# Keys' transposes moved to another PSUM ring, 34 copies moved from VectorE to ScalarE, and a new written-out order, in a one-core gated-recurrence and low-rank mixer kernel

## The chip, the cores and the metric

One core of one Trainium2 chip runs the whole program in one launch. The metric is the device time of an execution in microseconds (us). TensorE does the matrix products, VectorE (DVE in the profile), ScalarE (ACT) and GpSimd (POOL) do the elementwise work, and the queue of SyncE (SP) issues most of the transfers.

## The reference

The reference has two stages. The first is a recurrence with a complex gate over 768 tokens, for 4 batches x 8 heads with head size 48. The second mixes tokens with a rank-32 product and channels with a two-layer perceptron of width 1536.

```python
def _attn_ref(q, k, v, a_re, a_im):            # (4, 8, 768, 48) each
    mag = np.sqrt(a_re * a_re + a_im * a_im)
    scale = np.minimum(mag, 0.999) / (mag + 1e-06)
    a_re_n, a_im_n = (a_re * scale, a_im * scale)
    ...
    for t in range(S):
        ar, ai = (a_re_n[:, :, t, :, None], a_im_n[:, :, t, :, None])
        new_re = ar * S_re - ai * S_im
        new_im = ar * S_im + ai * S_re
        kv = np.einsum('bhd,bhe->bhde', k[:, :, t], v[:, :, t])
        S_re, S_im = (new_re + kv, new_im)
        y[:, :, t] = np.einsum('bhd,bhde->bhe', q[:, :, t], S_re)

def _moe_ref(x, U, V, w_ch1, w_ch2):           # x = y as (4, 768, 384)
    xt = x.transpose(0, 2, 1)
    h = xt @ U @ V
    u = x + h.transpose(0, 2, 1)
    ch = np.maximum(u @ w_ch1, 0.0) @ w_ch2
    return (u + ch).astype(np.float32)
```

## The kernel before, in words

The tokens are cut into 24 chunks of 128 (6 for each batch). Gates are worked out in 12 groups of two chunks, the mixer in 12 pieces of two chunks, numbered m = 0 to 11.

- `gates(g)` turns the gate of group g into logarithms of its size and into angles (ScalarE's tables, with VectorE between). From group 3 on (`SPLIT`) the logarithms and the angles are split into two parts for TensorE: one copy in the rounded type, in the tile `GS` (L658 for 768 columns, L772 for 384), and the remainder by a subtraction after it. Products with constant matrices (`es ps`, `ef ps`, `tot`, `ph`) then sum the parts along the tokens.
- `prep(i)` weighs the queries and keys of chunk i, then turns queries and keys in the procedure `turn` (L841): 16 small products each, from two halves of the array's rows into two PSUM tiles `tr`. ScalarE copies each of the two tiles out into `QK` (L852).
- `chain(i)` does the level products `inner` (L888, L891) and `corners` (L952), the state's update `dk` (L977), and the output products `y` (L1008, L1016). From group 5 on the `inner` products of two chunks are issued together.
- `mixer(m)` does the rank products (`rank`, `mixed`), transposes the mixed rows (`uTp`, L1088) and copies them into `uT` (chunk 0 of the piece by VectorE, L1094; chunk 1 by ScalarE, L1092), then multiplies with the weights: `up` (L1103) and `down` (L1336) for m up to 6, a form with fewer products, `few` (L1202), from m = 7 on.

PSUM has four rings of two buffers each. Their tags are `T` (gates' sums, all `tr` tiles, `rank`, `mixed`, `uTp`), `A` (`inner`, `corners`, some of `fix` and `few`), `Y` (`dk`, `y`) and `M` (`up`, `down`, `few`). A product that takes a buffer waits until the readers of the tile two takes earlier in its ring are done.

Nothing is reordered when the kernel runs. Every operation has a place in the table `ORDER`, written out by hand for each engine, kind and rank, and `Plan.order` sorts by place, so every engine has one fixed queue. TensorE's operations carry a number `way` for the layout in which the array is cut: 0 for the whole array, 1, 3, 5, 6 and 7 for layouts of smaller parts (`turn` and `mixed` have 5, `dk` and the first part of `y` 3, `inner`, `corners` and the second part of `y` 1, `up`, `down` and `few` 0).

`SPARE` names places ahead of which TensorE is given products of the identity that nothing reads (L1485, `up<-ident` and `down<-ident`); they write PSUM tiles of the ring `M` that are not in use yet. A unit is 128 columns, and up to four units make one product.

Of the kernel before, what the change touches and what calls it, by code (L numbers as in the profile page):

```python
# [19 lines left out]
HC = CH // 2  # L20
# [19 lines left out]
        ("POOL", "load"): {0: [21], 1: [43], 1.5: [38], 2: [22]},  # L40
        ("DVE", "load"): {1: [68]},
# [6 lines left out]
        ("ACT", "gates"): {0: [1, 4, 2, 6, 7, 11, 12, 13, 14, 42, 35, 49, 57, 60], 1: [25, 27, 37, 39, 40, 41, 48, 50, 53, 52, 56, 59], 2: [122, 101,  # L48
# [10 lines left out]
        ("DVE", "gates"): {0: [5, 8, 9, 15, 17, 66, 16], 1: [29, 44, 45, 46, 47, 67, 63], 2: [110, 140, 146, 179, 142], 4: [276, 311, 326, 359, 338],  # L59
# [10 lines left out]
        ("ACT", "angles"): {0: [75, 84, 89, 92, 95], 1: [77, 99, 108, 113, 114], 2: [210, 228, 250, 242, 245, 246, 267, 272, 275], 4: [378, 398, 416,  # L70
# [5 lines left out]
        ("DVE", "angles"): {0: [76, 88], 1: [82, 105], 2: [215, 236, 251], 4: [383, 399, 417], 6: [589, 598, 599, 609, 624, 625, 642], 8: [695, 714,  # L76
# [5 lines left out]
        ("DVE", "prep"): {0: [87, 96, 106], 1: [109, 119, 135], 2: [232, 249, 254], 3: [264, 278, 308], 4: [358, 415, 419], 5: [401, 454, 472], 6:  # L82
# [160 lines left out]
def kernel(  # L243
# [24 lines left out]
    nc = tc.nc  # L268
# [36 lines left out]
    BITS = range(SPLIT[0])  # L305
    PUT = (0, 2), (4, 6), (8, 10)

    AT_ONCE = (0, 1, 2)
    WP = 768

    def pool(name, bufs=1, **kw):
# [1240 lines left out]
```

## Time and profile before

| | us |
|---|---|
| median of 3 runs (lowest, highest) | 637.16 (634.21, 637.46) |
| the profiled execution, its own time | 638.28 |
| its span, first to last instruction | 636.5 |
| busy: TensorE products (PE) | 621.5 (98%) |
| busy: VectorE (DVE) | 513.8 (81%) |
| busy: ScalarE (ACT) | 401.2 (63%) |
| granted TensorE clock, mean | 0.994 |

PE is the row of products, PEld that of the weight loads, which overlap them. The busy time of PE is modelled, and a product that follows another of the same form starts long before the one ahead of it has ended, so a busy PE can still hide short delays. A row of the timeline gives the start, the length from the first start to the last end, the engine, the line and the count; a row of the chain of waits gives the stretch by which this work moved the end of the chain on. A line L383, L386 or L380 is a helper's, and such rows are told apart by their tiles.

### The profile page before, as it was taken

The page shows a single profiled execution, that of the slowest core. Times are in us where ns is not written, and L with a number is a line of the kernel's source. Part 1 is how long each engine was busy: PE and PEld are TensorE (multiplying, and loading weights), DVE is VectorE, ACT ScalarE, POOL GpSimd, SP SyncE. Part 2 cuts the span into 40 slices and gives each one's busy share as a digit, 9 for nine tenths or more (in the row PEclk, how much of TensorE's full clock was granted, in tenths as well). Part 3 has the DMA queues.
Part 4 walks back from the last instruction along what each step waited for, and adds up shares of the span by engine and source line. Part 5 has one row for each costly group of instructions (what it writes and reads, how often), then busy time and mean ns, then how long its engine had stood idle before and what let it go on. Part 6 is the DMA issues. An engine that isn't in the chain of part 4 may idle for free.

```text
span 636.5 us, 23451 instructions
## 1 busy us (share of the span) xinstructions
PE 621.5 (98%) x10376; PEld 527.6 (83%) x10376; DVE 513.8 (81%) x921; ACT 401.2 (63%) x773; POOL 39.7 (6%) x79
## 2 busy tenths in 40 slices
PE   7999998999999999999999999999999999999998
PEld 3567667755889989889889889788999998999997
DVE  7999997799999989758877977888998985464643
ACT  7999987898887787876776675768532431202010
POOL 5000000001001000010010100010000000000010
PEclk9999989999999999999999999999999999999999
DMA  8865544537232452522422422512122110000011
GB/s 201 182 159 136 123 111 113 129 101 162 44 72 52 80 103 46 98 59 45 85 57 47 91 45 42 113 44 37 34 61 34 25 35 2 1 1 13 1 38 50
DMA packets 173685, 45.74 MB, mean 72 GB/s; under 512 B 167632, under 2 KB 170384, under 8 KB 173584
## 3 DMA queue, kind: packets, MB, share of 16 engines
q1 hardware_dynamic: 171376, 39.90, 29.8%
q0 software_dynamic: 2208, 4.35, 2.0%
q8 instruction: 81, 1.33, 0.9%
q14 instruction: 20, 0.16, 0.1%
HBM read 33.59 MB, written 4.72 MB: 60 GB/s over the span
## 4 chain that ended last, share of the span: by engine, by line
PE 83%; issue 5%; DVE 4%; ACT 4%; DMA 2%; SPq 0%; POOL 0%; DVEq 0%; ACTq 0%; POOLq 0%
PE down L1336 24%; PE up L1103 17%; PE few L1202 11%; PE tr L841 4%; PE dk L977 4%; PE y L1016 4%; PE inner L891 3%; PE y L1008 2%; PE inner L888 2%; PE up L1485 2%; PE tot L726 2%; PE mixed L1070 1%; ACT gate L380 1%; PE uTp L1088 1%; PE es ps L678 1%
## 5 line engine op out<-in xcount | busy, mean ns | idle before, releaser
L1103 PE MATMUL up<-uT,w 128*128 128x256 f32 x504 | 119.1, 388 | 0.0
L383 DVE TENSOR_TENSOR QK<-QK,T 112x512 f32<-112x512 f32 (+2 forms) x144 | 103.0, 732 | 11.2 <-PE inner L888 4.3
L1103 PEld LDWEIGHTS up<-uT,w 128*128 128x128 f32 x504 | 94.5, 192 | 13.1
L1336 PE MATMUL down<-w,h 128*128 128x192 f32 x396 | 74.3, 332 | 0.0
L380 ACT ACTIVATE gate<-gate 128x768 f32<-128x768 f32 (+1 forms) x89 | 70.5, 798 | 4.6 <-DMA gate<-in_a_im_dram 1.8
L852 ACT COPY QK<-tr 112x512 f32<-112x512 f32 x96 | 53.2, 585 | 28.3 <-PE tr L841 27.6
L1336 PEld LDWEIGHTS down<-w,h 128*128 128x128 f32 x396 | 64.0, 190 | 2.7 <-issue 1.7
L383 DVE TENSOR_TENSOR QKC<-qk,cs 128x768 f32<-128x768 f32 x48 | 45.6, 955 | 10.6 <-PE dk L977 5.6
L1210 ACT COPY h<-few 128x512 f32<-128x512 f32 x30 | 17.3, 586 | 53.9 <-PE few L1202 53.9
L386 DVE TENSOR_TENSOR xo<-down,xo 128x192 f32<-128x192 f32 (+1 forms) x79 | 30.4, 387 | 21.1 <-PE down L1336 21.0
L1336 PE MATMUL down<-stage 128*128 128x192 f32 x198 | 37.6, 331 | 0.0
L841 PEld LDWEIGHTS tr<-ident,QKC 64*112 64x112 f32 x768 | 26.0, 130 | 12.7 <-issue 5.2
L1202 PE MATMUL few<-gate,w 128*128 128x128 f32 x280 | 36.3, 277 | 0.0
L841 PE MATMUL tr<-ident,QKC 64*112 64x64 f32 x768 | 33.1, 222 | 1.9 <-ACT QK L852 1.7
L1278 POOL DMA_DIRECT2D out_dram<-xo x32 | 18.8, 608 | 254.7 <-DVE xo L386 143.6
L1202 PEld LDWEIGHTS few<-gate,w 128*128 128x128 f32 x280 | 34.0, 192 | 0.2
L1485 PE MATMUL up<-ident 128*128 128x512 f32 (+3 forms) x82 | 31.0, 488 | 2.3 <-POOL ident masks.py:199 1.4
L764 POOL DMA_DIRECT2D gate<-F x15 | 12.4, 827 | 325.2 <-DVE F L789 203.5
L1336 PEld LDWEIGHTS down<-stage 128*128 128x128 f32 x198 | 32.0, 190 | 0.7 <-issue 0.2
L380 ACT ACTIVATE h<-up 128x512 f32<-128x512 f32 x42 | 24.8, 596 | 11.2 <-PE up L1103 10.9
L377 ACT ACT_TABLE_LOAD x24 | 30.8, 1283 | 1.1 <-PEq L1536 0.7
L957 ACT COPY AT<-corners 32x128 f32<-32x128 f32 x96 | 24.3, 255 | 10.6 <-PE corners L952 9.2
(168 smaller groups left out, 1255.7 us busy)
## 6 DMA issues: line engine op xcount, KB each, us to landing
stage<-in_moe_w_ch_dram SPq DMA_DIRECT2D x12, 768.0 KB, 4.9
gate<-in_a_im_dram SPq DMA_DIRECT2D x24, 192.0 KB, 3.7
gate<-in_a_re_dram SPq DMA_DIRECT2D x24, 192.0 KB, 3.5
qk<-in_q_dram SPq DMA_DIRECT2D x24, 192.0 KB, 3.2
qk<-in_k_dram SPq DMA_DIRECT2D x24, 192.0 KB, 3.3
VP<-in_v_dram SPq DMA_DIRECT2D x24, 192.0 KB, 3.3
AT<-DG SPq DMA_DIRECT2D x96, 32.0 KB, 2.3
T<-E SPq DMA_DIRECT2D x48, 48.0 KB, 2.9
```

The lines of the kernel that those rows point to most:

```text
L377: ACT(1.37, rank, lambda: nc.scalar.preload_act_table_set(name), writes=[TABLE])
L380: return nc.scalar.activation(out=o, in_=i, func=f, **kw)
L383: nc.vector.tensor_tensor(out=o, in0=a, in1=b, op=OP.mult)
L386: nc.vector.tensor_tensor(out=o, in0=a, in1=b, op=OP.add)
L841: nc.tensor.transpose(out=get(*ps[r])[0:DQ, h], in_=get(*qkc)[at, h].rearrange("p u d -> p (u d)")[:, 0:DQ], identity=ident[at, at], tile_ ...
L852: nc.scalar.copy(out=to, in_=a)
L977: nc.tensor.matmul(out=get(*dk[r])[x:end, h], lhsT=get(*ks)[at, h, x // DP, 0:end - x], rhs=get(*VPi)[at, h], start=True, stop=True, tile_ ...
L1016: nc.tensor.matmul(out=get(*y[u])[side(r, u), p], lhsT=k_of(h, r * HC, HC), rhs=get(*(mid_G if r else ("G", i - 1)))[:, h], start=False, s ...
L1103: nc.tensor.matmul(out=get(*ps)[:, e], lhsT=w1[:, f, (ff + e) * 128:(ff + e + 1) * 128], rhs=get(*uT)[:, f], start=(f == 0), stop=(f == KD ...
L1202: nc.tensor.matmul(out=get(*ps)[:, q], lhsT=w()[:, q * 128:(q + 1) * 128], rhs=v[0](), start=(n == 0 and q == 0), stop=True, skip_group_ch ...
L1336: nc.tensor.matmul(out=get(*to)[:, part], lhsT=x(j), rhs=y[:, j], start=(first and j == 0), stop=(j == KH - 1), skip_group_check=not first)
L1485: nc.tensor.matmul(out=to[:, 0:k * 128].rearrange("p (k m) -> p k m", k=k), lhsT=ident, rhs=ident.unsqueeze(1).to_broadcast([128, k, 128]) ...
```

## The change

Four things are changed.

1. In `prep`, the two PSUM tiles of the keys' transposes come from the ring `A`; the queries' stay in `T`.
2. In `gates` and `angles`, the rounded copies into `GS` are made by ScalarE for groups 4 to 11 (8 copies of 768 columns, 16 of 384).
3. In `turned`, chunk 0 of the pieces m = 2 to 11 is copied into `uT` by ScalarE too (10 copies).
4. `ORDER` and `SPARE` are new as a whole. The set of operations is the same, apart from the engine of the 34 copies. `SPARE` has 127 units at 47 places where it had 120 at 36.

The code, and of the tables the rows of the transposes and the spare products:

```diff
-        ("PE", "prep"): {0: [107, 115], 1: [129, 148], 2: [260, 266], 3: [294, 319], 4: [420, 435], 5: [458, 480], 6: [725, 703], 7: [749, 776], 8:
-        [876, 913], 9: [927, 969], 10: [1059, 1078], 11: [1118, 1132], 12: [1305, 1299], 13: [1318, 1332], 14: [1452, 1473], 15: [1510, 1521], 16:
-        [1706, 1691], 17: [1739, 1727], 18: [1881, 1856], 19: [1911, 1895], 20: [2083, 2066], 21: [2096, 2110], 22: [2277, 2266], 23: [2290, 2297]},
+        ("PE", "prep"): {0: [115, 117], 1: [131, 153], 2: [268, 274], 3: [311, 310], 4: [419, 424], 5: [475, 476], 6: [730, 714], 7: [767, 768], 8:
+        [882, 914], 9: [921, 983], 10: [1073, 1084], 11: [1124, 1123], 12: [1299, 1271], 13: [1310, 1311], 14: [1470, 1477], 15: [1510, 1517], 16:
+        [1668, 1709], 17: [1708, 1736], 18: [1874, 1868], 19: [1905, 1899], 20: [2078, 2076], 21: [2105, 2104], 22: [2273, 2272], 23: [2302, 2304]},
...
-SPARE = {34: 19, 36: 1, 51: 11, 55: 2, 79: 7, 97: 1, 107: 9, 115: 2, 117: 3, 129: 1, 148: 14, 151: 2, 154: 2, 169: 1, 183: 1, 201: 2, 212: 4, 260: 6,
...
+SPARE = {33: 13, 34: 8, 50: 8, 85: 7, 115: 11, 128: 2, 151: 8, 153: 4, 172: 1, 179: 5, 202: 4, 224: 1, 237: 1, 242: 1, 246: 1, 247: 1, 249: 1, 268: 2,
...
     AT_ONCE = (0, 1, 2)
+    MADE = range(4, NG)
     WP = 768
...
                 a, b = ("gs0", g), ("gs1", g)
-                DVE(c_one(W), R1, lambda: nc.vector.tensor_copy(out=get(*a), in_=t(l)), [L], [a])
+                if g in MADE:
+                    ACT(ca, R1, lambda: nc.scalar.copy(out=get(*a), in_=t(l)), [L], [a])
+                else:
+                    DVE(c_one(W), R1, lambda: nc.vector.tensor_copy(out=get(*a), in_=t(l)), [L], [a])
...
                 a, b = ("zs0", g), ("zs1", g)
-                DVE(c_one(DM), R2, lambda: nc.vector.tensor_copy(out=of(a, i), in_=of(z, i)), [zi], [a + (i,)])
+                if g in MADE:
+                    ACT(c_act(DM), R2, lambda: nc.scalar.copy(out=of(a, i), in_=of(z, i)), [zi], [a + (i,)])
+                else:
+                    DVE(c_one(DM), R2, lambda: nc.vector.tensor_copy(out=of(a, i), in_=of(z, i)), [zi], [a + (i,)])
...
             for r in range(2):
-                psum(ps[r], "T", [128, H, HC])
+                psum(ps[r], "A" if u else "T", [128, H, HC])
...
-            if cc:
+            if cc or m > 1:
                 ACT(c_act(DM) - 0.045, R0, lambda: nc.scalar.copy(out=to(), in_=get(*tr)), [tr], [uT + (cc,)])
             else:
                 DVE(c_dve(DM), R0, lambda: nc.vector.tensor_copy(out=to(), in_=get(*tr)), [tr], [uT + (cc,)])
```

More of the change, by code (lines that the diff above doesn't have):

```diff
@@ L30 @@
 ORDER = {
[9 rows of a table removed]
-        ("POOL", "load"): {0: [21], 1: [43], 1.5: [38], 2: [22]},
-        ("DVE", "load"): {1: [68]},
[6 rows of a table removed]
-        ("ACT", "gates"): {0: [1, 4, 2, 6, 7, 11, 12, 13, 14, 42, 35, 49, 57, 60], 1: [25, 27, 37, 39, 40, 41, 48, 50, 53, 52, 56, 59], 2: [122, 101,
[10 rows of a table removed]
-        ("DVE", "gates"): {0: [5, 8, 9, 15, 17, 66, 16], 1: [29, 44, 45, 46, 47, 67, 63], 2: [110, 140, 146, 179, 142], 4: [276, 311, 326, 359, 338],
[10 rows of a table removed]
-        ("ACT", "angles"): {0: [75, 84, 89, 92, 95], 1: [77, 99, 108, 113, 114], 2: [210, 228, 250, 242, 245, 246, 267, 272, 275], 4: [378, 398, 416,
[5 rows of a table removed]
@@ L76 @@
-        ("DVE", "angles"): {0: [76, 88], 1: [82, 105], 2: [215, 236, 251], 4: [383, 399, 417], 6: [589, 598, 599, 609, 624, 625, 642], 8: [695, 714,
[5 rows of a table removed]
-        ("DVE", "prep"): {0: [87, 96, 106], 1: [109, 119, 135], 2: [232, 249, 254], 3: [264, 278, 308], 4: [358, 415, 419], 5: [401, 454, 472], 6:
[6 rows of a table removed]
-        ("ACT", "prep"): {0: [111, 112, 121, 120], 1: [141, 131, 149, 150], 2: [265, 261, 269, 270], 3: [298, 309, 324, 322], 4: [431, 430, 437, 438],
[4 rows of a table removed]
-        ("DVE", "rest"): {0: [116, 166, 171, 192, 134, 159, 176], 1: [177, 231, 238, 262, 214, 237, 243, 263], 2: [271, 321, 328, 355, 282, 295, 312,
[8 rows of a table removed]
@@ L103 @@
-        ("DVE", "levels"): {0: [128, 136, 167, 137, 144, 168], 1: [172, 190, 200, 185, 191, 223], 2: [274, 293, 327, 292, 303, 342], 3: [343, 361,
[9 rows of a table removed]
-        ("ACT", "levels"): {0: [147], 1: [211], 2: [313], 3: [379], 4: [470], 5: [508], 6: [769], 7: [851], 8: [948], 9: [1008], 10: [1160], 11:
[14 rows of a table removed]
-        ("ACT", "rest"): {0: [187, 204, 195, 194, 216, 218, 221], 1: [257, 255, 259, 268, 283, 285, 286], 2: [341, 332, 368, 363, 395, 389, 394], 3:
[10 rows of a table removed]
-        ("ACT", "small"): {0: [594, 291, 418, 489, 340, 521, 590, 593, 622, 630], 1: [748, 822, 791, 799, 771, 856, 878], 2: [985, 1087, 1141, 1121,
[4 rows of a table removed]
@@ L144 @@
-        ("DVE", "small"): {0: [244, 596, 631, 638, 644, 684, 685, 686, 602, 604, 741, 733], 1: [694, 734, 693, 830, 823, 852, 880, 904, 905, 920, 935,
[26 rows of a table removed]
-        ("POOL", "small"): {0: [1036, 870], 1: [1115, 1046, 1047], 2: [1408, 1257, 1310], 3: [1516, 1525, 1526], 4: [1703, 1688, 1719], 5: [2001,
-        1888, 2009], 6: [2140, 2080, 2141], 7: [2340, 2327, 2328], 8: [2638, 2635, 2666], 9: [2627, 2629, 2636], 10: [2628, 2634, 2637]},
-        ("POOL", "angles"): {6: [618], 8: [712, 736], 10: [873, 921], 12: [1114], 14: [1260, 1297], 16: [1467, 1500], 18: [1687], 20: [1889, 1921],
@@ L174 @@
-        22: [2045, 2068]},
-        ("DVE", "mixing"): {7: [2021, 2029, 2027, 2030, 2107, 2022, 2028, 2088, 2097, 2113, 2132, 2133, 2059]},
-}
-SPARE = {34: 19, 36: 1, 51: 11, 55: 2, 79: 7, 97: 1, 107: 9, 115: 2, 117: 3, 129: 1, 148: 14, 151: 2, 154: 2, 169: 1, 183: 1, 201: 2, 212: 4, 260: 6,
-         266: 2, 284: 2, 288: 1, 310: 1, 354: 1, 371: 1, 376: 1, 397: 1, 400: 2, 420: 1, 458: 2, 466: 3, 471: 4, 497: 1, 524: 1, 595: 3, 603: 2, 623:
-         3}
[9 rows of a table added]
+        ("POOL", "load"): {0: [16], 1: [31], 1.5: [28], 2: [27]},
@@ new lines @@
+        ("DVE", "load"): {1: [69]},
[6 rows of a table added]
+        ("ACT", "gates"): {0: [1, 2, 4, 6, 7, 10, 11, 19, 49, 35, 46, 47, 66, 67], 1: [23, 25, 39, 40, 42, 43, 48, 55, 52, 53, 54, 64], 2: [135, 111,
[10 rows of a table added]
+        ("DVE", "gates"): {0: [5, 8, 9, 12, 14, 59, 13], 1: [26, 21, 41, 44, 45, 70, 61], 2: [124, 139, 156, 194, 149], 4: [267, 319, 326, 353, 325],
[10 rows of a table added]
+        ("ACT", "angles"): {0: [68, 87, 101, 104, 105], 1: [79, 107, 113, 114, 125], 2: [212, 232, 252, 240, 241, 245, 261, 262, 264], 4: [380, 398,
[5 rows of a table added]
+        ("DVE", "angles"): {0: [77, 94], 1: [81, 108], 2: [217, 234, 255], 4: [386, 400, 412], 6: [585, 600, 604, 617, 621, 624, 637], 8: [698, 721,
[4 rows of a table added]
@@ new lines @@
+        ("DVE", "prep"): {0: [74, 106, 109], 1: [112, 130, 150], 2: [221, 253, 266], 3: [199, 296, 306], 4: [355, 410, 413], 5: [434, 452, 471], 6:
[6 rows of a table added]
+        ("ACT", "prep"): {0: [116, 121, 123, 122], 1: [145, 148, 157, 155], 2: [271, 272, 279, 278], 3: [320, 316, 315, 317], 4: [437, 438, 439, 440],
[4 rows of a table added]
+        ("DVE", "rest"): {0: [118, 154, 158, 185, 129, 184, 190], 1: [165, 208, 235, 263, 220, 243, 250, 254], 2: [283, 318, 328, 358, 280, 323, 341,
[8 rows of a table added]
+        ("DVE", "levels"): {0: [127, 133, 146, 132, 134, 152], 1: [173, 187, 188, 186, 189, 210], 2: [284, 292, 304, 291, 293, 309], 3: [329, 345,
[9 rows of a table added]
@@ new lines @@
+        ("ACT", "levels"): {0: [140], 1: [195], 2: [303], 3: [349], 4: [465], 5: [510], 6: [762], 7: [829], 8: [954], 9: [1014], 10: [1158], 11:
[14 rows of a table added]
+        ("ACT", "rest"): {0: [193, 191, 204, 192, 216, 226, 215], 1: [256, 258, 259, 257, 277, 275, 276], 2: [367, 340, 365, 366, 390, 391, 392], 3:
[10 rows of a table added]
+        ("ACT", "small"): {0: [595, 282, 312, 488, 393, 508, 607, 614, 622, 628], 1: [741, 808, 775, 813, 784, 847, 857], 2: [993, 956, 1110, 1142,
[4 rows of a table added]
+        ("DVE", "small"): {0: [248, 601, 632, 634, 642, 636, 679, 672, 609, 612, 743, 753], 1: [695, 747, 691, 836, 830, 831, 861, 873, 899, 916, 933,
[25 rows of a table added]
@@ new lines @@
+        ("POOL", "small"): {0: [816, 925], 1: [1113, 1103, 1163], 2: [1305, 1358, 1359], 3: [1511, 1474, 1516], 4: [1694, 1690, 1783], 5: [1975, 1886,
+        1976], 6: [2137, 2134, 2135], 7: [2363, 2282, 2372], 8: [2586, 2585, 2587], 9: [2641, 2588, 2628], 10: [2639, 2646, 2647]},
+        ("POOL", "angles"): {6: [620], 8: [713, 739], 10: [878, 930], 12: [1104], 14: [1267, 1307], 16: [1462, 1512], 18: [1676], 20: [1855, 1910],
+        22: [2020, 2091]},
+        ("DVE", "mixing"): {7: [2015, 2018, 2048, 2049, 2057, 2024, 2029, 2113, 2114, 2115, 2112, 2126, 2051]},
+}
@@ L183 @@
+SPARE = {33: 13, 34: 8, 50: 8, 85: 7, 115: 11, 128: 2, 151: 8, 153: 4, 172: 1, 179: 5, 202: 4, 224: 1, 237: 1, 242: 1, 246: 1, 247: 1, 249: 1, 268: 2,
+         274: 1, 281: 1, 285: 2, 286: 1, 310: 1, 336: 2, 338: 1, 344: 5, 369: 1, 376: 1, 378: 1, 394: 1, 408: 1, 418: 1, 419: 5, 424: 1, 431: 1, 442:
+         2, 469: 2, 472: 1, 503: 1, 519: 1, 596: 2, 602: 1, 610: 3, 619: 1, 623: 3, 627: 1, 640: 3}
 class Plan:
```

244 rows, old and new, of the table ORDER are left out of this document.

## The prediction

> **What bounds the kernel now.** I read first the busy time by stretches. Its columns are the stretch, its length, then busy us (and instructions) of PE, PEld, DVE, ACT and POOL, the granted clock, the DMA share and GB/s.
>
> ```profile
> 0.00:160.00 160.00, 148.90 (x2426) 98.67 (x2426) 142.15 (x234) 141.44 (x260) 12.39 (x35) 0.98 0.60 141
> 160.00:260.00 100.00, 99.69 (x2153) 88.83 (x2152) 94.33 (x162) 81.50 (x159) 5.79 (x9) 1.00 0.36 71
> 260.00:460.00 200.00, 199.39 (x3513) 174.22 (x3512) 159.60 (x280) 140.45 (x271) 13.97 (x21) 1.00 0.30 60
> 460.00:540.00 80.00, 80.00 (x1597) 73.67 (x1596) 66.43 (x132) 26.14 (x63) 2.72 (x5) 1.00 0.15 32
> 540.00:636.50 96.50, 93.48 (x697) 92.26 (x695) 51.25 (x116) 11.68 (x21) 4.80 (x9) 1.00 0.05 17
> ```
>
> There are two stages. Up to 160 us VectorE and ScalarE are each busy 88 to 89%, and TensorE idles 11.1 us although identity products fill another 31.0 us of it (L1485 among the costliest groups): here the elementwise work sets the pace. From 160 us to the last product TensorE idles about 1 us. The waits of PE from 160 to 633 us agree, they are three in all:
>
> ```profile
> PE inner L891 <- issue: 0.3, 1, 0.3
> PE y L1008 <- ACT gate L380: 0.3, 1, 0.3
> PE tr L841 <- ACT QK L852: 0.2, 1, 0.2
> ```
>
> So after 160 us only what shortens TensorE's own queue shortens the run. What its queue loses is not in idle time but in the products themselves. I read it in the chain of waits, in order of time (start, us, what):
>
> ```profile
> 160.92 1.07 PE dk L977 x57
> 161.99 0.59 PE tr L841 x16
> 162.58 2.79 PE up L1103 x12
> 165.37 0.35 PE ph L778 x2
> 165.72 2.59 PE up L1103 x12
> 168.31 0.59 PE tr L841 x16
> 168.90 0.62 PE inner L888 x51
> 169.52 2.79 PE up L1103 x12
> ```
>
> The same twelve products of `up` move the chain by 2.59 us behind whole-array work (`ph`) and by 2.79 us behind work in small parts (`tr`, `inner`). Coming back to the whole array therefore costs 0.20 us. Sixteen `tr` products take 0.59 us whether they follow `dk` or `up`.
>
> **Part 1, the order and the ring A.** I read TensorE's queue off both tables, operation by operation, with each one's `way`. The whole queue changes layout 282 times before and 264 times after. Up to the first `inner` of chunk 6 (160 us) both have 77 changes; from there on 205 become 187: into small parts from the whole array 77 to 74, back to the whole array 78 to 75, from one small layout to another 50 to 38. The reason is the ring: the keys' `turn` no longer needs the two T buffers that the queries' `turn` has just filled, and among the 34 `turn`s of the later stage there are now 13 places where two stand side by side, where there was none.
>
> Price of a change: back to the whole array 0.20 us (2.79 - 2.59). Into small parts: in the timeline the row of 16 `tr` products is 0.66 us long, its last product 0.22 us (the group's mean is 222 ns), so the 16 starts spread over 0.44 us, 0.03 us a step. A run behind its own kind would move the chain by 16 x 0.03 = 0.47 us, not 0.59: a change costs 0.12 us. Sum: 3 x 0.20 + (3 + 12) x 0.12 = 0.60 + 1.80 = **-2.4 us**, all of it on the path, since nothing else is awaited there. Bounds: if a second `turn` streams no faster than a first, the 12 changes between small layouts give nothing and -1.0 is left; if every change cost 0.20, -3.6. I take -2.4, the rows being of these very operations.
>
> Does the new ring add waits? `A` now carries 34 more tiles of the late stage. Their readers are two ScalarE copies of 585 ns (`QK`), `copy_predicated` of 294 and 443 ns, and four ScalarE copies of 255 ns (`AT`, 1.02 us together). Summing the rows of the TensorE work that stands between a tile's last product and the next take of its buffer, less its readers' rows, one take in `A` keeps 0.3 us to spare and all others over 1.2 us. In `T` the takes with under 1 us to spare fall from 44 to 24. So I put this at 0; if the cover went, a chunk would lose what its readers are late (the second rival).
>
> **Part 2, the start.** All `turn`s there and the spare products are re-placed. What the ring can save is seen in the waits of `tr`:
>
> ```profile
> PEld tr L841 <- ACT QK L852: 4.1, 9, 0.8
> ```
>
> Of the 4.1 us, 0.6 lie after 160 us, so 3.5 us at most in the start, behind ScalarE's copies of the queries. One of them has a sequel:
>
> ```profile
> 85.56 0.26 PE L841 MATMUL tr<-ident,QKC 64*112 64x64 f32 x1 [0.68 <-ACT QK L852]
> ...
> 86.64 4.54 PE L1103 MATMUL up<-uT,w 128*128 128x256 f32 x12
> ```
>
> That `up` is 1.7 us longer than the 2.86 us of the one at 162.51, in a stretch whose granted clock is 0.91. Bound of the gain: 3.5 + 1.7 = 5.2 us. But TensorE has slack here and VectorE and ScalarE do not, so a wait of TensorE that goes is mostly made up of waiting for them later. The three moved copies of group 4 fall in this stage: ScalarE gets 841 + 2 x 518 ns = 1.9 us, VectorE loses 558 + 2 x 355 ns = 1.3 us. From 120 to 160 us both are at 92% and more. The spare products grow by 7 units; 31.0 us for the bulk of 120 units is 0.26 us each, +1.8 us if they met no idle time, 0 if they do, as TensorE's 11.1 idle us let me expect. Bounds for the start: -5.2 to +3.7 us; I take 0, because elementwise work there changes by under 1%.
>
> **Part 3, copies after 160 us.** VectorE loses 7 x 558 + 14 x 355 + 10 x 552 ns = 14.4 us; ScalarE gains 7 x 841 + 14 x 518 + 10 x 478 ns = 17.9 us. The rows for VectorE, from the groups of instructions (busy us, mean ns of one, idle time before):
>
> ```profile
> L1094 DVE COPY uT<-uTp 128x384 f32<-128x384 f32 x12 | 6.6, 552 | 3.1 <-PE uTp L1088 3.1
> ...
> L772 DVE CAST GS<-gate 128x384 fp32r<-128x384 f32 x18 | 6.4, 355 | 2.9 <-DMA gate<-F 2.9
> ...
> L658 DVE CAST GS<-GL 128x768 fp32r<-128x768 f32 x9 | 5.0, 558 | 0.6 <-PE ph L778 0.3
> ```
>
> ScalarE's prices are from ACT rows of the same size (`gate` 768 columns 841, `cs` 384 columns 518, `uT` from PSUM 478). ScalarE is 70 to 82% busy from 160 to 460 us and can take this; VectorE's relief is worth nothing while TensorE does not wait for it. On the path is only `uT`: both halves now come one after the other, 2 x 478 = 0.96 us and not 0.55 side by side, so `up` or `few` gets its input 0.4 us later. Behind these copies on ScalarE stand the copies of `QK` and `h`; they wait with them if `uTp` is late. In the new order the TensorE work between the last `uTp` and the first product of `uT` is 0.9 to 1.0 us for m = 4 and 6 and 1.95 us (with VectorE's sums between) for m = 9 and 11; elsewhere it is 1.4 us and more. Four times up to 0.4 us: 0 to +1.6, I take +0.4.
>
> The Trainium skill speaks against this part: TensorEngine Tiling (Array Packing), section PSUM Bottleneck, asks for both ScalarE and VectorE to empty PSUM. By that rule all ten pieces would lose; the trace shows no product waiting for either copy (no waiter under L1092 or L1094), and which of the two holds here decides the third rival.
>
> **The sum.** -2.4 + 0 + 0.4 = -2.0 us. On the profiled execution, 638.28 us (span 636.5 and 1.8 around it), that is 636.3. The profile lies 1.1 us above the median, so the median goes from 637.16 to **635.1**; 0.5% is 3.2 us, about what a measurement of this kernel can tell from no change, so 634.0 and 640.3 are the bounds of "same".
>
> **The rivals.** *The start gets shorter too* (0.24). The waits behind `QK` and the half-speed stretch after them go, and VectorE and ScalarE follow: 4 of the 5.2 us, 631. For it: these waits are what the ring removes. Against: both engines are over 88% busy there.
>
> *The ring A holds TensorE up* (0.09, slower). Every chunk's keys wait in `A` for the readers of `corners` or `inner` on VectorE, 94% busy from 160 to 260 us. It decides from 5.2 us (2.0 + 3.2), 0.31 us for each of 17 chunks; at 0.5 us each it costs 8.5, giving 644. Against: the cover of 1.2 us and more.
>
> *The serial copies and ScalarE's load eat the gain* (0.16). Ten pieces at 0.4 us are +4.1 in place of +0.4, or the start pays ScalarE's 1.9 and part of the spare units: 637 to 639, no change.
>
> *Transposes side by side slow the clock* (0.03, slower). Thirteen pairs, each followed by a half-speed `up` at +1.7 us, 22 us, 657. The Trainium skill, TensorE: Matmul & The Clock Gate, Part 4, says that transposes do not count as busy for the gate. Against: a pair lasts 1.1 us, and the clock is 1.00 from 160 to 540 us with all its `tr`.
>
> **How the numbers follow.** The forecast itself has 0.48, its own range 633 to 637.5; about 0.14 of it lies under 634.0. Faster: 0.14 + 0.24 = 0.38. Slower: 0.09 + 0.03 = 0.12. Same: 0.34 + 0.16 = 0.50. The range that leaves out the slower cases and the lowest of the first rival is 630.5 to 640.0.
>
> **What would show it.** Right: from 160 us to the last product PE busy as before, 13 `tr` rows of x32 in the timeline, the stage about 2.4 us shorter, the start within 2 us of 160. Wrong: new waits of `tr` or `inner` on DVE or ACT rows after 160 us; `up` or `few` waiting for ACT `uT`; a `tr` x32 row longer than 1.2 us; a start that moved by more than 3 us, which would mean that I mis-sized the re-placed elementwise work.

## The result: 641.47 us, slower by 0.8%

After ran in 641.47 us (median of 10 runs, 638.82 to 642.85), before on the same chip in 637.29 us (10 runs). The ratio is 1.0078, 95% interval 1.0054 to 1.0101. The forecast was 635.1, its range 630.5 to 640.0. The profiled execution of after took 642.85 us, its span is 641.0.

First the same stretches as before, with two short ones of the start between them (stretch, length, busy us and instructions of PE, PEld, DVE, ACT and POOL, granted clock, DMA share, GB/s):

```profile
0.00:160.00 160.00, 144.19 (x2397) 99.00 (x2398) 135.46 (x225) 137.64 (x252) 12.15 (x34) 0.97 0.60 140
120.00:130.00 10.00, 7.33 (x102) 5.34 (x102) 5.71 (x10) 7.82 (x12) 0.00 (x0) 0.82 0.96 230
130.00:140.00 10.00, 8.81 (x54) 4.38 (x54) 4.55 (x9) 5.67 (x9) 0.96 (x1) 0.84 0.63 158
160.00:260.00 100.00, 98.64 (x2017) 85.80 (x2016) 88.81 (x148) 84.33 (x160) 6.03 (x9) 1.00 0.33 65
260.00:460.00 200.00, 199.99 (x3584) 176.14 (x3584) 155.17 (x266) 150.69 (x296) 13.46 (x21) 1.00 0.32 62
460.00:540.00 80.00, 80.00 (x1684) 75.20 (x1684) 68.08 (x136) 30.86 (x75) 3.84 (x7) 1.00 0.17 35
540.00:641.00 101.00, 97.97 (x738) 95.12 (x730) 51.61 (x117) 13.31 (x25) 4.83 (x9) 1.00 0.05 17
```

Up to 160 us VectorE has done 6.7 us less work and ScalarE 3.8 us less than in before (142.15 and 141.44). Most of the loss sits between 120 and 140 us: there VectorE is busy for 10.3 of 20 us, and TensorE's clock is 0.82 to 0.84. From 160 us on TensorE is as busy as before. Its waits from 160 us to the last product (one row, in place of three of 0.2 to 0.4 us):

```profile
PE ph L783 <- ACT QK L857: 1.4, 1, 1.4
```

To put a time on each stretch I gave every TensorE operation the time that it usually takes in before, and looked up when each profile has done the first so many us of that work. The table gives this as a difference from the profile of before (us; minus is earlier; 110 us of work are done at 164.5 us in before, 550 us at 616.3, and nothing changes after that). The rows below "after" are the experiments.

| work done | 50 | 70 | 90 | 110 | 230 | 410 | 550 |
|---|---|---|---|---|---|---|---|
| after | +3.1 | 0.0 | +6.1 | +8.4 | +7.3 | +4.5 | +4.5 |
| e1_late | -0.1 | -3.0 | -3.0 | +1.6 | -0.8 | -3.7 | -3.7 |
| e1_again | +0.2 | -2.8 | -2.8 | -0.6 | -2.8 | -5.7 | -5.7 |
| e2_start | +3.2 | +0.8 | +5.2 | +6.4 | +6.1 | +10.2 | +10.7 |
| e3_back | +3.1 | +0.5 | +6.1 | +9.1 | +8.4 | +16.6 | +16.9 |
| e4_r | +4.0 | +1.9 | +8.0 | +9.5 | +8.4 | +6.0 | +5.9 |
| e5_carry | +5.0 | +3.1 | +7.3 | +7.9 | +6.5 | +3.7 | +3.7 |
| e6_both | +3.1 | +1.3 | +3.3 | +5.4 | +4.5 | +1.7 | +1.6 |
| e7_split | 0.0 | -3.9 | -3.8 | -2.6 | +0.2 | +1.1 | +2.2 |
| e8_zs | -0.2 | -2.4 | -1.9 | -0.6 | -2.2 | -4.1 | -3.9 |
| e9_dve | -0.1 | -3.9 | -3.8 | -3.0 | -5.1 | +3.9 | +4.2 |
| e10_cover | 0.0 | -1.8 | -1.3 | +0.5 | -1.8 | -4.7 | -4.7 |
| e11_copies | -0.1 | -1.7 | -1.6 | +0.4 | +3.6 | +5.9 | +5.9 |
| f1_middle | +2.7 | +1.8 | +2.8 | +3.6 | +2.4 | -0.5 | -0.6 |
| f2_from585 | +0.6 | +3.0 | +8.3 | +9.7 | +7.4 | +4.5 | +4.4 |

So after loses 8.4 us in the start and gains 3.9 us between 110 and 410 us of work. The column at 110 depends on how the work is weighed: with the median step from one product's start to the next as its time, this column is 1.1 to 1.2 us lower for every kernel with after's late order (after +7.2, e1_late +0.4) and the same for e2_start and e11_copies, while the other columns agree within 0.5 us. By these weights the late gain of after is 2.7 us. (At 70 the kernels with before's start are 1.7 to 3.9 us ahead of before's own profile, which had a stretch at half clock at 111 us; differences of 2 us between single profiles mean little.)

A part is lost early. At 50 us of work (about 86 us in before) the seven kernels with after's first 584 places are 2.7 to 5.0 us behind, and all others within 0.6 us of before. In this stretch the new `SPARE` puts spare products ahead of products that are awaited (the same ten us of before and of after, then two rows of after's timeline):

```profile
70.00:80.00 10.00, 9.37 (x239) 6.23 (x238) 9.99 (x16) 9.50 (x22) 0.00 (x0) 1.00 0.60 125
70.00:80.00 10.00, 10.00 (x246) 6.95 (x245) 8.48 (x15) 8.04 (x18) 0.00 (x0) 1.00 0.54 122
73.94 1.24 PE L1490 MATMUL up<-ident 128*128 128x512 f32 x4
75.87 0.49 ACT L379 ACTIVATE gate<-ef ps 128x384 f32<-128x384 f32 x1 [0.85 <-PE ef ps L684]
```

After has 3.6 us of spare products here, before none. TensorE never idles, while VectorE and ScalarE do 1.5 us less each. The products `tot` of the third group start at 76.61 us in after and at 73.65 us in before. In the 5.3 us ahead of them stand four rows of spare products, which take 2.2 us of TensorE's queue. No run leaves these spare products out, so that they cost the 3 us is argued from rows and not shown.

The larger part is lost later, first on TensorE (timeline of after: start, us, engine, line, tiles, count, idle time ahead and its releaser):

```profile
121.75 2.14 PE L1056 MATMUL rank<-xo,UV 128*32 128x384 f32 x24
126.57 1.49 PE L1121 MATMUL rT<-fold,r 64*128 64x32 f32 x6 [2.67 <-ACT r L1062]
127.87 2.18 PE L1075 MATMUL mixed<-r,V 64*128 64x192 f32 x8
131.51 3.60 PE L1130 MATMUL rw ps<-w,rw 128*32 128x512 f32 x24
```

`rank` of piece 0 is done at 123.9 us, but its copy `r` stands in ScalarE's queue behind a weight conversion that waits for its load, so `rT` starts at 126.57 (before: 124.78). The two spare units placed ahead of `rT` are not issued, since the PSUM tiles that they would write are still to be read by copies of `h` that the new order has put later. Behind this idle stretch the clock is at half for 6.8 us (126.4 to 133.2 us in the trace's record of the clock): `rw ps` takes 3.60 us, in before 2.77.

Then the second wait (timeline of after, the rows around the carry row of chunk 6, which POOL's transfer adds to the first row of chunk 7's angles):

```profile
131.80 0.56 DVE L794 SCALAR_TENSOR_TENSOR F<-F,ph 128x384 f32<-128x384 f32 x1 [0.29 <-ACT F L379]
132.99 0.96 POOL L766 DMA_DIRECT2D gate<-F  x1 [120.69 <-DVE F L794]
133.29 0.37 SPq L550 DMA_DIRECT2D stage<-in_moe_w_ch_dram  x1
137.99 0.36 DVE L777 CAST GS<-gate 128x384 fp32r<-128x384 f32 x1 [4.76 <-DMA gate<-F]
```

The carry row is 1.5 KB. It is issued at 132.99, a weight load of 768 KB 0.30 us later, and `zs0` of chunk 7 can start 5.0 us after the issue; VectorE stands for 4.76 us with everything behind it. In before the weight load comes 1.29 us after the carry row (129.77 and 131.06), the row is there at 131.80 at the latest, and VectorE has `qk` of chunk 6 to do meanwhile. The trace's records of the DMA packets say where the time goes: the row's own packets begin 3.9 us after its issue in after, 1.5 us after it in before.

### The profile page after: what moved, and what is told of

Same layout as the page of the kernel before. It is cut to its first block, busy times and chain, and to the rows that moved or that the text cites. A ratio compares the mean times of both kernels' runs of the same rounds, so it can differ in the third digit from the quotient of the medians.

```text
span 641.0 us, 23499 instructions
## 1 busy us (share of the span) xinstructions
PE 620.8 (97%) x10400; PEld 531.3 (83%) x10400; DVE 499.1 (78%) x887; ACT 416.8 (65%) x807; POOL 40.3 (6%) x79
## 4 chain that ended last, share of the span: by engine, by line
PE 86%; ACT 4%; DVE 3%; DMA 3%; issue 2%; SPq 1%; ACTq 0%; DVEq 0%
PE down L1341 24%; PE up L1108 17%; PE few L1207 11%; PE dk L982 4%; PE tr L846 4%; PE y L1021 3%; PE inner L896 3%; PE up L1490 3%; PE y L1013 2%; PE inner L893 2%; PE down L1298 2%; PE tot L728 2%; ACT gate L379 2%; PE mixed L1075 1%; PE uTp L1093 1%
## 5 line engine op out<-in xcount | busy, mean ns | idle before, releaser
L1108 PE MATMUL up<-uT,w 128*128 128x256 f32 x504 | 116.2, 383 | 0.0
L857 ACT COPY QK<-tr 112x512 f32<-112x512 f32 x96 | 51.8, 592 | 16.8 <-PE tr L846 16.6
L1490 PE MATMUL up<-ident 128*128 128x128 f32 (+3 forms) x104 | 35.8, 448 | 1.4 <-POOL ident masks.py:199 1.4
L1097 ACT COPY uT<-uTp 128x384 f32<-128x384 f32 x22 | 10.1, 481 | 38.0 <-DVE more L1333 15.1
L908 DVE COPY_PREDICATED DG<-mask,inner 128x128 f32<-128x128 int32 (+1 forms) x72 | 23.8, 341 | 12.7 <-PE inner L896 6.2
L962 ACT COPY AT<-corners 32x128 f32<-32x128 f32 x96 | 24.3, 256 | 12.2 <-PE corners L957 10.7
```

Source lines behind the costliest of these rows:

```text
L857: nc.scalar.copy(out=to, in_=a)
L962: ACT(0.36, RR, lambda r=r, u=u: nc.scalar.copy(out=get(*ATi).rearrange("p (a u) t -> p a u t", u=2)[r:r + BLK, :, u, BLK:2 * BLK], in_=ge ...
L1108: nc.tensor.matmul(out=get(*ps)[:, e], lhsT=w1[:, f, (ff + e) * 128:(ff + e + 1) * 128], rhs=get(*uT)[:, f], start=(f == 0), stop=(f == KD ...
L1490: nc.tensor.matmul(out=to[:, 0:k * 128].rearrange("p (k m) -> p k m", k=k), lhsT=ident, rhs=ident.unsqueeze(1).to_broadcast([128, k, 128]) ...
```

## The experiments

The theory: the loss is the new order of the start, between 120 and 157 us, the gain of the late stage is real and comes from fewer changes of layout. Medians of runs on the same chip as before's; the ratios, with their 95% intervals, are to before, and are not exactly the quotients of the two medians.

**e1_late and e2_start: the halves.** e1_late has before's order up to place 740 and after's behind it; e2_start the opposite.

```diff
 e1_late, against after (and before's order up to place 740)
-    MADE = range(4, NG)
+    MADE = range(5, NG)
-                psum(ps[r], "A" if u else "T", [128, H, HC])
+                psum(ps[r], "A" if u and i >= 7 else "T", [128, H, HC])
 e2_start, against after (and before's order from place 740 on)
-    MADE = range(4, NG)
+    MADE = (4,)
-                psum(ps[r], "A" if u else "T", [128, H, HC])
+                psum(ps[r], "A" if u and i < 7 else "T", [128, H, HC])
-            if cc or m > 1:
+            if cc:
```

> The first 740 places in the order of before with its spare products, with all transposes of chunks 0 to 6 in ring T and group 4 copied by VectorE as before; everything after place 740 in the order of after, with the keys of chunks 7 to 23 in ring A and the copies of groups 5 to 11 and of uT for m = 2 to 11 on ScalarE. Theory (the loss lies in the new order of the start, between 120 and 157 us, and the late stage of after gains 3 to 4 us by fewer changes of layout): this kernel keeps the gain without the loss, 633.5, some 3.8 under before, range 632 to 635. Rival S (the late stage of after only makes up slack that its late start gave it): 637, as before. Rival R (ring A or the copies on ScalarE cost time late, and the start is a symptom): 640 to 641, as after.

> The complement: the first 740 places in the order of after with its spare products, keys of chunks 0 to 6 in ring A and group 4's copies on ScalarE; everything after that in the order of before, keys in T, copies on VectorE. Theory: the loss of the start (8.3 us at 157 us) without the gain of the late stage, 644 to 646. Rival S: the late stage makes up some 4 of the 8 us in either order, 641. Rival R: the late stage is as before, 637.

Measured: e1_late 633.99 us (before 637.94), ratio 0.992 (0.9893 to 0.9947); e2_start 646.38 us, ratio 1.0121 (1.0083 to 1.0158). Both as the theory had it (e2_start 0.4 us above its range): the halves go apart in opposite directions, -0.8% and +1.2%. Not all of e2_start's loss is the start. Its profile, of the slowest of its nine runs (649.07), is 6.4 us behind at 110 us of work and loses some 4 us more near 405 us, where TensorE waits 1.4 us for a placing transfer (`AT<-DG`) and the clock is then at half for 6.8 us. That the late stage only makes up slack (S) and that ring or copies cost time late (R) are both out.

**e3_back: all 34 copies back on VectorE, order and ring as in after.**

```diff
-    MADE = range(4, NG)
+    MADE = ()
-            if cc or m > 1:
+            if cc:
```

> The order, the spare products and the ring A of after, but all 34 copies back on VectorE at the same places in the order. Theory: the copies are off the path, 641 within 1.5 (group 4's copies stand after the place of the loss; the serial copies of uT cost at most 0.4 us each in four pieces, so at best 1.6 less). Rival R (ScalarE's extra load of 1.9 us in the start and 17.9 us late is what after pays): 637.

Measured: 652.62 us, ratio 1.022 (1.0184 to 1.0257), 1.4% over after. Neither theory had this: the copies are not indifferent, their move to ScalarE is needed by the new order. By the table 7 us of it are lost in one place, between 250 and 270 us of work, where `zs0` of chunk 16 waits in VectorE's queue for its carry row. e8_zs and e9_dve below take this up.

**e4_r, e5_carry, e6_both: the two waits repaired one by one.** Only the queues named change. In them `cx` and `w2` are conversions of weights, `h` is a copy out of `up`, `r` the copy out of `rank`, and `zs0` and `zs1` are the rounded copy and the remainder of a chunk's angles:

```diff
 e4_r, ScalarE's queue behind y of group 3
-  cx 9, r, n 8, w2 9, x 8, h(0,8), F 6, table, h(0,10), ...
+  h(0,8), h(0,10), r, cx 9, n 8, w2 9, x 8, F 6, table, ...
 e5_carry, VectorE's queue behind F 6
-  w2 9, zs0 7, zs1 7, h(0,0), ...
+  zs0 7, zs1 7, w2 9, h(0,0), ...
 e6_both: e4_r's queue, and VectorE's behind F 6
-  w2 9, zs0 7, zs1 7, ..., prep 6 qk
+  prep 6 qk, zs0 7, zs1 7, w2 9, ...
```

> After with one repair in ScalarE's queue: the copies h of piece 0 (rows 8 and 10) and then the copy r stand ahead of the weight conversion cx 9, which waits 1.3 us for its load, so r ends near 125.4 instead of 126.5 and the spare products ahead of rT find their PSUM tiles free. Theory: r 1.1 us earlier, no idle stretch of 3 us on TensorE and so no half-speed stretch of 6.8 us behind it (rT, mixed and rw ps cost 1.9 us more there): 2 to 3 us less at 132 us. If the carry row's transfer then no longer meets the weight load, up to 6 us less. 636 to 639 in the end. Rival C (the carry transfer that waits behind the weight load at 133 us sets everything, and what comes ahead of it has slack): 641.

> After with one operation moved in VectorE's queue: the weight conversion w2 that frees the stage buffer now stands behind the pair zs0, zs1 of chunk 7, which waits for the carry row (1.5 KB from POOL). The 768 KB weight load, which needs that buffer and was issued 0.3 us after the carry row's transfer, then comes 5 us later. Nothing else is moved, so VectorE still waits. Theory K (the carry row is slow because the weight load is in the DMA engines with it): from POOL's issue to zs0 about 2.5 us in place of 5.0, zs0 at 135.5 in place of 138.0, and 2 to 3 us less in the end: 638 to 640. Rival (the row takes 5 us by itself in this order, or the wait has slack behind it): 641 to 642.

> After with the moves of e4_r and e5_carry together, and the product of queries and keys with es (prep 6, 0.95 us) put ahead of zs0 of chunk 7 as cover on VectorE. Theory (two waits one behind the other: r behind the weight conversion, then the carry row behind the weight load): the first mixer's steps come 1.3 us earlier by the one and 2.5 us earlier by the other, and 0.9 us of VectorE's work fits into what is left: 4 to 5 us less than after, 636.5 to 638. Rival (each repair only uncovers the next wait, as e4_r did): 640 to 642.

e4_r: 642.30 us (before 637.94), ratio 1.0067 (1.0035 to 1.0098): nothing gained, rival C. Its timeline:

```profile
126.49 0.70 PE L1505 MATMUL down<-ident 128*128 128x256 f32 x2 [0.88 <-ACT h L394]
127.35 0.85 PE L1136 MATMUL rT<-fold,r 64*128 64x32 f32 x6 [0.16 <-ACT r L1077]
138.25 0.36 DVE L792 CAST GS<-gate 128x384 fp32r<-128x384 f32 x1 [4.84 <-DMA gate<-F]
```

The spare products are there again and `rT` runs at full speed, but `zs0` of chunk 7 starts at 138.25, as late as in after, 5.1 us behind its transfer's issue. The first wait had the second behind it.

e5_carry: 639.72 us (before 635.69), ratio 1.0063 (1.0036 to 1.009). Its timeline:

```profile
134.38 0.96 POOL L781 DMA_DIRECT2D gate<-F  x1 [122.88 <-DVE F L809]
136.38 0.36 DVE L792 CAST GS<-gate 128x384 fp32r<-128x384 f32 x1 [2.63 <-DMA gate<-F]
137.25 0.95 DVE L584 SCALAR_TENSOR_TENSOR w<-stage,w 128x768 uint32<-128x768 uint32 x1
138.26 0.37 SPq L565 DMA_DIRECT2D stage<-in_moe_w_ch_dram  x1
```

With the weight load 3.9 us behind it the carry row takes 2.0 us, not 5.0, and its packets begin 1.5 us after the issue, as in before. That settles the mechanism K, for the weight load together with the transfers behind it in SyncE's queue, which came later with it. What VectorE does meanwhile is not the cause: in before it works through the whole transfer, which is as short. The time follows in the profile alone (this execution came 1.9 us later to the place than after's, and left it 0.5 us earlier); the ratio can't be told from after's.

e6_both: 638.65 us (before 635.69), ratio 1.0045 (1.0018 to 1.0072). The carry row takes 2.0 us again (132.60 to 134.60), `zs0` starts 3.4 us earlier than in after, and the profile ends 2.9 us earlier. The forecast of 4 to 5 us was too much, and 5.4 of the 8.4 us at 110 us of work are still there. The interval of the ratio overlaps that of after (1.0054 to 1.0101), so the gain is read from the profile.

**f1_middle and f2_from585: where the rest is.**

```diff
 f1_middle
+  after's order to place 584, before's from there to its place 740, after's behind it
-    MADE = range(4, NG)
+    MADE = range(5, NG)
 f2_from585
+  before's order to place 585, after's behind it
-                psum(ps[r], "A" if u else "T", [128, H, HC])
+                psum(ps[r], "A" if u and i >= 5 else "T", [128, H, HC])
```

> After, with its order replaced only in the middle: places 0 to 584 as after (to 122 us, with SyncE's 14.2 us behind a placing transfer at 102 us), then what before has up to its place 740, then the order of after; group 4's copies on VectorE, all keys in ring A. Theory (the 8 us are lost in the order of places 585 to 740: the carry row behind the weight load, r behind the conversion, and what stands behind them): as e1_late, 0.992 to 0.997 of before, 632 to 635. Rival P (the loss is prepared before 122 us, by the weight loads that come 13 us late): 638 to 642.

> The complement: before's order up to place 585, after's from there on, copies on ScalarE from group 4 on, keys of chunks 5 to 23 in ring A. Theory: the loss is in it, 1.004 to 1.010 of before, 639 to 643. Rival P: 632 to 635.

f1_middle: 638.08 us (before 637.49), ratio 1.0009 (0.9991 to 1.0028). f2_from585: 640.98 us, ratio 1.0056 (1.0032 to 1.0079). f2 is as the theory had it: with before's first places, places 585 to 740 alone carry a loss. f1 missed the theory's range and lies at the lower end of P's: with before's middle after's first 122 us still cost 0.6 to 0.9% against e1 (0.992 and 0.995). Its interval lies under that of after, so the middle costs time too, and P holds in part. The parts don't add up: 0.006 to 0.009 for the early part alone, 0.011 to 0.014 for the middle alone, 0.013 to 0.016 for both. In f1's trace ScalarE still waits 1.4 us for a weight load at 132 us. Which operation before 122 us costs the time was not taken apart; it stays open. The table dates its loss: f1 is 2.7 us behind already at 50 us of work, where the rows above show the spare products. In the trace of after SyncE's queue stands, later than that, for 14.2 us behind a transfer that places level products (until 102 us, and the weight load behind it is issued at 107.2 where before issued it at 94.3).

**e7_split: 13 pairs of transposes separated again,** one of each pair moved past one or two neighbouring TensorE operations in e1_late.

```diff
 TensorE's queue, for instance chunk 7
-  tr(7,0), tr(7,1), up(1,0), ...
+  tr(7,0), up(1,0), tr(7,1), ...
```

> The kernel of e1_late with 13 pairs of transposes side by side separated again (chunks 7 to 23): one of each pair is moved past one or two neighbouring products of TensorE, nothing else. TensorE's queue changes layout 287 times in place of 264: 5 more into small parts from the whole array, 5 more back, 13 more between small layouts. Theory (the late gain of 4.2 us is TensorE's changes of layout): 5 x 0.20 + 18 x 0.12 = 3.2 us more than e1_late, 636.5 to 638. Rival (the late gain comes from the copies that left VectorE): within 1 us of e1_late, 633.5 to 635.

Measured: 645.07 us (before 635.69), ratio 1.0128 (1.0088 to 1.0169), 1.8 to 2.1% over e1_late, about four times the forecast. Its five runs fall into 640.4 (two) and 645.1 (three), and the profile is of one of the short ones (640.45). From 110 us of work to the end the profile loses 4.8 us where e1_late gains 5.3. Some 4.7 us of these 10.1 are idle time of TensorE (longest row below); it is the sum of 100, 100, 100 and 80 us less the busy time from 160 to 540 us, 4.74, against 0.06 in e1_late. The other 5.4 us, where 3.2 were forecast, lie in busy time and were not traced to rows. The moved transposes came too late for their readers:

```profile
PE inner L911 <- DVE QK L397: 2.5, 2, 1.6
```

So this run can't give the price of a change. The rows do: from the start of the last product ahead to the first behind it, a run of 16 `tr` between two `up` takes 0.90 us in before, a run of 32 takes 1.35 us in after, and an `up` follows another by 0.22 us (2.59 / 12). Two runs cost 2 x (0.90 - 0.22) = 1.37 us, one double run 1.13: a pair saves 0.24 us; 13 pairs would save 3.1 us, an estimate, since the other pairs stand between other products. The second 16 of a double run add 0.45 us (1.35 - 0.90).

**e8_zs and e9_dve: which copies the new order needs.** Both are e1_late with copies back on VectorE: all but `zs0` in e8_zs, `zs0` too in e9_dve.

```diff
 e8_zs
-                if g in MADE:
+                if 0:
                     ACT(ca, R1, lambda: nc.scalar.copy(out=get(*a), in_=t(l)), [L], [a])
-            if cc or m > 1:
+            if cc:
 e9_dve, on top of it
-    MADE = range(5, NG)
+    MADE = ()
```

> The kernel of e1_late with only the 14 copies zs0 of groups 5 to 11 still on ScalarE; the 7 copies of 768 columns (gs0) and the 10 of uT are back on VectorE at the same places. e3_back, with all 34 back, lost 11 us against after, 7 of them where zs0 of chunk 16 stood 3.3 us in VectorE's queue for its carry row, ahead of the state's update. Theory Z (it is the wait for the carry row that must not stand in VectorE's queue; gs0 and uT are of no account): 634 to 635.5. Rival (VectorE's load as such, or uT side by side, decides): 639 to 645.

> The kernel of e8_zs with its last 14 moved copies, zs0 of groups 5 to 11, back on VectorE too, so that only the order and the ring A are left of the late stage's change. Theory Z (with zs0 on VectorE the wait for the carry row stands ahead of the state's update in VectorE's queue and TensorE waits for that, then runs at half clock): 5 to 11 us more than e8_zs, 639 to 645, the loss at chunk 16 as in e3_back. Rival (e3_back lost by gs0 and uT, or by the start): within 1.5 us of e8_zs, 633 to 636.

e8_zs: 634.47 us (before 635.69), ratio 0.9981 (0.9946 to 1.0015); its profile gains what e1_late's does, but the ratio is not clear of 1. e9_dve: 643.87 us (before 636.96), ratio 1.0129 (1.0078 to 1.018), 1.5% over e8_zs. The loss is where theory Z put it. Timeline of e9_dve, then its stretch from 310 us:

```profile
309.55 0.36 DVE L791 CAST GS<-gate 128x384 fp32r<-128x384 f32 x1 [3.43 <-DMA gate<-F]
309.82 0.55 DVE L399 TENSOR_TENSOR GM<-GM,dk 112x384 f32<-112x384 f32 x1
310.42 0.31 PE L1027 MATMUL y<-VP,AT 64*64 64x48 f32 x2 [1.99 <-DVE GM L399]
311.68 1.20 PE L1027 MATMUL y<-VP,AT 64*64 64x48 f32 x30 [0.94 <-DVE G L399]
```

```profile
310.00:320.00 10.00, 8.64 (x108) 8.11 (x109) 5.38 (x9) 2.91 (x6) 0.00 (x0) 0.54 0.31 61
```

The copy waits 3.43 us for its carry row, the state's update `GM` stands behind it on VectorE, TensorE waits for that, and then the clock is at half (0.54): 2.9 us of waiting cost 7.0 (read off between 250 and 270 us of work; the table's step from 230 to 410, 9.0, has later waits in it as well). In e8_zs the same waits stand on ScalarE, 8.8 us of them, and no product is late by them (the group of these copies):

```profile
L790 ACT CAST GS<-gate 128x384 fp32r<-128x384 f32 x14 | 7.2, 516 | 8.9 <-DMA gate<-F 8.8
```

**e11_copies: the 34 copies alone,** order, spare products and rings as before.

```diff
+    MADE = range(4, NG)
-            if cc:
+            if cc or m > 1:
```

> Before with the 34 copies alone on ScalarE: order, spare products and rings as before. Theory: the copies by themselves bring nothing, since TensorE waits for nothing in the late stage of before (three waits, 0.8 us in all); 637, within 1.5 us. Rival (the copies are the gain): 633 to 634. Rival (ScalarE's queue, in an order not made for it, holds up the copies of QK and h): 640 and more.

Measured: 645.46 us, ratio 1.0138 (1.0107 to 1.0169). The third rival: in an order that was not made for it ScalarE holds up what it empties for TensorE (waits of PE from 150 us on; before has one such row of 0.2 us):

```profile
PE tr L861 <- ACT QK L872: 2.1, 3, 1.1
PE tr L861 <- ACT gate L394: 2.0, 1, 2.0
```

**e1_again and e10_cover: the better kernel, and a cover for its own carry row.**

```diff
 VectorE's queue
-  zs0 8, zs1 8, w2s, ...
+  w2s, zs0 8, zs1 8, ...
 TensorE's queue
-  ph 8, down 0, ...
+  down 0, ph 8, ...
```

> The kernel of e1_late unchanged, on the chip of this comparison, as the reference for the three others: 0.992 of before again, within 0.003.

> The kernel of e1_late with work put in front of its own wait for a carry row (zs0 of chunk 8 stood 2.55 us in VectorE's queue at 153 us, TensorE idle 2.3 us, then a stretch at half clock): the copy w2s (1.35 us, VectorE) stands ahead of zs0 and zs1 of chunk 8, and one down (four products, TensorE) ahead of ph of chunk 8. Theory K (a carry row costs what is not covered of its 2 to 6 us): 1 to 3 us less than e1_late, the wait of zs0 under 1.3 us. Rival (the wait has slack behind it): e1_late within 0.7 us.

e1_again: 633.04 us (before 636.96), ratio 0.995 (0.9921 to 0.9979), at the edge of what was expected. e10_cover: 633.88 us, ratio 0.9954 (0.9934 to 0.9974): no gain, where 1 to 3 us were expected, though the wait of `zs0` is gone from its profile (1.63 us in e1_again). VectorE then waits 1.15 us for `F` instead, which came later by the products put ahead of `ph`. e1_late is faster than before by 0.5 to 0.8%, and so faster than after too.

## Why the prediction was wrong, point by point

**The step that failed is Part 2, "I take 0, because elementwise work there changes by under 1%".** I priced amounts of work where the queues' order decides. Its upper bound, +3.7, was built from busy times alone; measured are +7.2 to +8.4 in the profile of after (by the weights of the table), and +6.4 in that of e2_start, which has after's start alone. What I had named as the sign of this ("a start that moved by more than 3 us") came. I had not followed the moved conversions on ScalarE's queue past `r`, nor the weight load on SyncE's queue past POOL's carry row. Both orders were in the two tables. By e6_both these two waits are some 3 us of it; f1_middle puts another part, 2.7 us at 50 us of work, before 122 us, and its cause stays open.

**Spare products at 0 to +1.8 us:** wrong in kind, as I priced their number and not their places. Those placed ahead of `rT` cost nothing, as they were not issued, and the idle stretch then had half clock behind it; with them back (e4_r) the time was the same, so neither side was worth anything there. Those at 71 to 76 us stand ahead of awaited products and take 2.2 us of TensorE's queue; that this is the early loss is likely by the rows and not shown by a run.

**Part 1, -2.4 us (bounds -1.0 to -3.6):** the rows bear the mechanism out, and the size can't be told to be wrong. The second 16 `tr` of a double run add 0.45 us, where I had 0.47. A pair between two `up` saves 0.24 us, where my prices give 0.32 (0.20 and 0.12). Between 110 and 410 us of work after gains 3.9 us and the other kernels with this late stage and `zs0` on ScalarE 3.5 to 5.3; by the second weights these are 2.7 and 2.3 to 4.1. No run gives the changes of layout alone: e7_split, which was to do so, has waits in it.

**The ring A at 0:** right. TensorE's one wait after 160 us is `ph`, which takes a tile of `T`; none is for a tile of `A`. There are 13 rows like this first one of the chain (start, us, what):

```profile
175.14 1.08 PE tr L846 x32
176.22 2.79 PE up L1108 x12
```

A double run moves the chain by 1.08 us. In the timeline the 13 rows are 1.10 to 1.15 us long, under the 1.2 that I had set as the limit, and the `up` behind this one takes the usual 2.79. So the rival of the slowed clock is out as well: the clock is 1.00 from 160 to 540 us. The rule of the Trainium skill (TensorE: Matmul & The Clock Gate, Part 4) that transposes don't count as busy in the same way had no effect at this length.

**Part 3:** "VectorE's relief is worth nothing while TensorE does not wait for it" is true of before, where I read it, and false of the new order, which leans on it: e9_dve loses 1.5% against e8_zs. That ScalarE "can take this" is true in the new order and false in that of before, where the 34 copies cost 1.4% (e11_copies). For `uT` the forecast of +0.4 can't be told from nothing. The rule that asks for both engines to empty PSUM (the Trainium skill, TensorEngine Tiling (Array Packing), section PSUM Bottleneck) would have the ten `uT` copies lose on ScalarE; e8_zs, which has them (and seven copies of 768 columns) back on VectorE, gains nothing by it.

**The rivals:** none of the four was it. The slower one that I gave (ring A, 644) came near in time for a wrong reason.

## What to carry to other kernels

When an order is searched anew, its cost is not in the sums of busy time: walk each in-order queue at the places where something waits for a transfer, and ask what stands behind it and what large transfer was issued beside it. A copy that waits for a transfer belongs on the queue whose next work nobody awaits; which engine that is depends on the order, so engine and order have to be judged together (in the late stage the order without the copies was 1.3% slower than before, the copies without the order 1.4%, the pair 0.5 to 0.8% faster). Where a change has an early and a late part, build the two halves crosswise: two runs showed a gain of 0.8% (0.5% when repeated) inside a loss of 0.8%.

## What the runs showed of the hardware

- A 1.5 KB transfer from POOL took 2.0 us when 768 KB were issued 1.3 us after it or later (before, e5_carry, e6_both; 2.3 in f1_middle) and 4.9 to 5.1 us when they were issued 0.3 us after it (after, e2_start, e3_back, e4_r, f2_from585). In the second case its own packets began 3.8 to 4.0 us after the issue, in the first 1.5 us. The Trainium skill (DMA: Bandwidth & Descriptors, section Queues, rings and completion order) says that a DMA engine takes turns between its queues packet by packet; by that rule alone the small one should have passed early, and here it came only as the load ended (in e2_start the load landed at 136.9 us, the row at 137.1). The 2.0 us agree with the fixed cost of roughly 2 us for every transfer that the Trainium skill gives in SBUF — State Buffer, section The DMA setup-cost knee.
- Most waits of TensorE of 2 to 3 us had a stretch at half clock behind them: 2.67 us in after at 126 us, 2.06 and 0.94 us in e3_back at 322 us, 1.99 and 0.94 us in e9_dve at 310 us. By the clock column after then lost 3.4 us (0.82 and 0.84 in two stretches of 10 us), e9_dve 5.1 (0.54 from 310 to 320 us, 0.95 in the ten behind it), so that wait and slow clock together came to 2.3 and 2.7 times the wait. It is no rule: in e11_copies a wait of 2.05 us at 281 us had the clock at 1.00 behind it, and in e2_start one of 1.37 us at 403 us had 6.8 us at half clock.
